# Gate and up projections of a gated MLP by Strassen's seven-product scheme, one Trainium2 core

## The chip, the cores and the metric

One core of a Trainium2 chip runs one launch. The metric is device time in microseconds (us), median of the runs shown. Engines are named as the profile names them: PE (matrix multiply; its weight loads are PEld), DVE (vector), ACT (scalar, activations), POOL (GpSimd), SP (the queue that issues every DMA here). `L326` is line 326 of the kernel before.

## The reference, cut to what matters

A transformer block with modulated layer norms: attention over 2048 queries, then a gated MLP. All values are float32. With D = 576, F = 4608 and 2048 tokens:

```python
mod = (silu(c) @ w_mod).reshape(1, 6, 1, -1)      # sa, ca, ga, sb, cb, gb
h = layernorm(x) * (1 + ca) + sa
x = x + ga * attention(h, k_cache, v_cache, wq, wo)  # 32 heads, 16 kv heads, last 512 keys
h = layernorm(x) * (1 + cb) + sb
gate = h @ W_gate                                  # (2048, 576) @ (576, 4608)
up = h @ W_up
x = x + gb * ((gate * (gate > 0) * up) @ W_down)
```

## The kernel before

**Precision.** PE multiplies in fp32r, a float32 format cut short. Every operand is therefore kept as two parts, hi (a cast on ACT) and lo (the rest, a subtraction on POOL), and a product is made as hi·hi + hi·lo + lo·hi, accumulated in PSUM. `split` (L173, L174) does this for weights.

**Projections.** `proj_ops` (L326) lists the matmuls of one 128 x 512 result (128 features, 512 tokens) with D = 576 as contraction: four tiles of 128 rows, three matmuls each, and the last 64 rows, whose hi and lo lie one above the other, in two. That is 14 matmuls of 512 columns. The operand of one 512-token block is `hT[qb]`, nine 512-column tiles in one buffer.

**Attention.** 128 units `u`, each one head and 512 queries. One unit's stages are written out by hand in the loop at the end, with steps of other work (`step(name, t, fn)`, due times shifted by the table `PLAN`) run between them. PE, DVE, ACT and POOL keep the order of the program. `T.*` and `woT*` are the last unit's leftovers, after `e = 10 * NU`. `b0` to `b3` are the second layer norm of the four 512-token blocks: statistics, norm on ACT, transposes on PE (L284), and `affine`, which writes hi and lo straight into `hT`.

**MLP.** 72 units `m`: 18 pairs of 128-feature tiles (`g`) by 4 token blocks (`qb`). `glu_pieces` makes gate and up of two feature tiles (4 x 14 matmuls) in eight pieces; the last piece of each feature tile also takes the PSUM pair out: relu on ACT (L540), times up on DVE (L541), hi cast on ACT (L544), lo on POOL (L545). The down projection of the unit before runs between: `md_piece` calls `down_piece` (L501), 12 matmuls of 288 columns for one 128-token tile into `psW`, which has one buffer of two banks, and a DVE add into `acc` (L507). There are four such pieces to a unit, one behind each of the pieces 3 to 6:

```python
for i in range(8):
    if pcs:
        pcs[i]()
    if 3 <= i <= 6 and m > 0:
        md_piece(m - 1, i - 3)
```

The first MLP pieces run among the leftovers of attention, from the due time `e + MLP0`. Weights are loaded whole (one DMA for a 128-feature tile, `prep5`, L181), cut once, and used for four token blocks. PSUM: `psS` two pairs of banks, `psW` one pair, `psM` two single banks.

Of the kernel before, what the change touches and what calls it, by code (L numbers as in the profile page):

```python
# [26 lines left out]
PLAN = {'a1.st0': -14, 'a1.nm0': -15, 'a1.st1': -14, 'a1.nm1': -15, 'a1.st2': -14, 'a1.nm2': -15, 'a1.st3': -14, 'a1.nm3': -15, 'a1.rs': -15, 'a1.tr0': -15, 'a1.af0': -11, 'a1.tr1': -15, 'a1.af1': -15, 'a1.tr2': -15, 'a1.af2': -15, 'a2.tr2': -1, 'wo2.g': 2, 'a3.st0': -10, 'a2.st2': -10, 'wq2.c': 4, 'wo2.l': -2, 'wo2.c': -2, 'mods': -3, 'k1.l': -5, 'k1.c': -8, 'b3.st0': 9, 'b3.nm0': 4, 'b3.st1': 8, 'b3.nm1': 5, 'b3.st2': 1, 'b3.nm2': 2, 'b3.st3': 5, 'b3.nm3': 3, 'b3.rs': 4, 'b3.tr0': 4, 'b3.af0': 14, 'b3.tr1': 3, 'b3.af1': 7, 'b3.tr2': 4, 'b3.af2': 4, 'b2.st1': 6, 'woT-1.3': 5, 'b0.st2': 6, 'b1.st0': 6, 'b1.st1': 0, 'b1.st2': 5, 'b1.st3': 0, 'b1.rs': 4, 'woT-1.1': 6, 'b2.st0': 0, 'b2.af0': 2, 'b0.st0': 15, 'b0.st1': 4, 'b0.st3': 6, 'b1.nm0': 0, 'b1.tr1': -3, 'b2.tr2': -3, 'b0.rs': 4, 'b1.af1': 2, 'T.olo2': 1, 'b1.nm1': 7, 'gb': -12, 'wu0.l': -4, 'wu0.c': 4, 'wu1.l': -14, 'T.ohi2': 0, 'b1.nm3': 4, 'wu1.c': 2, 'b2.st3': 1, 'woT-3.1': 2, 'b2.nm1': 3, 'wg0.c': -4, 'wg1.l': -3, 'b1.nm2': -2, 'b2.nm2': 1, 'wg0.l': -3, 'b2.af1': 5, 'wd1.g': -4, 'woT-3.2': -6, 'wd1.c': -2, 'T.pv1': -4, 'b2.st2': -1, 'T.pv0': -3, 'b1.af0': 1, 'b0.tr0': -1, 'wg1.c': 1, 'T.sum': -1, 'wd0.l': -1, 'b0.nm0': 1, 'b0.nm1': 6, 'b0.nm2': 0, 'b0.nm3': 1, 'b2.nm3': 2}  # L27
CFG = {'a3': (('m', 'aav', 'vap'), ('w', 'vvv', 'aav'), ('w', 'vvp')), 'a2': (('m', 'aav', 'vvv'), ('w', 'vvv', 'vvv'), ('s', 'aap')), 'a0': (('s', 'vvp', 'vvv'), ('m', 'aap', 'avp'), ('w', 'aav')), 'a1': (('w', 'aap', 'vap'), ('m', 'vvp', 'vvv'), ('s', 'avp')), 'b2': (('m', 'aav', 'avp'), ('s', 'aap', 'vvv'), ('w', 'vap')), 'b0': (('w', 'aav', 'avv'), ('m', 'aav', 'avv'), ('s', 'vap')), 'b1': (('s', 'vav', 'avp'), ('m', 'aap', 'vvv'), ('s', 'avp')), 'b3': (('m', 'vvp', 'vvv'), ('s', 'avv', 'avp'), ('s', 'vap'))}
# [4 lines left out]
def kernel(  # L33
# [19 lines left out]
    hp = ctx.enter_context(tc.tile_pool(name="hp", bufs=NQB))  # L53
# [9 lines left out]
    psM = ctx.enter_context(tc.tile_pool(name="psM", bufs=2, space=bass.MemoryType.PSUM))  # L63
    psW = ctx.enter_context(tc.tile_pool(name="psW", bufs=1, space=bass.MemoryType.PSUM))

# [10 lines left out]
    # quad[p, j] = 1 where p and j agree modulo 32; mask[p, a] = 1 where p // 32 == a  # L76
# [10 lines left out]
    # minus[p, j] = -1 in the rows 0 and 16, which carry the two parts of the maximum  # L87
# [116 lines left out]
    def prep_out(d, k, src, key):  # L204
        st = {}

        def load():
            st["raw"] = rp.tile([P, 640], F32, tag="raw", name=f"ro{key}_{k}")
            nc.sync.dma_start(st["raw"][:, :D], src[k])

        def gate():
            raw = st["gated"] = st["raw"][:, :D]
            nc.vector.tensor_tensor(raw, raw, mods[key], op=ALU.mult)

        def cut():
            raw = st["gated"]
            d[k] = wp.tile([P, 2, D], F32R, tag="wC", name=f"wo{key}_{k}")
            split(raw, D, d[k][:, 0, :], d[k][:, 1, :])

        return load, gate, cut  # L220
# [4 lines left out]
    hT = [None] * NQB  # L225

# [8 lines left out]
    class LayerNorm:  # L235
# [51 lines left out]
        def affine(self, ds, pool, tag, engs):  # L287
            qb = self.qb
            if not self.ready:
                hT[qb] = hp.tile([P, 9, 512], F32R, tag="hT", name=f"hT{self.key}_{qb}")  # L290
# [5 lines left out]
            for j, (d, e) in enumerate(zip(ds, engs)):  # L296
# [7 lines left out]
                out[d] = (h[:, 8, :], h[64:, 8, :]) if d == 4 else (h[:, d, :], h[:, 4 + d, :])  # L304
# [11 lines left out]
    def proj_ops(ps, w, h):  # L316
        ops = []
        for t in range(4):
            ops.append((w[:, t, :], h[:, t, :]))
            ops.append((w[:, 5 + t, :], h[:, t, :]))  # L320
        ops.append((w[:, 4, :], h[:, 8, :]))
        ops.append((w[:, 9, :], h[:, 8, :]))
        for t in range(4):
            ops.append((w[:, t, :], h[:, 4 + t, :]))
        n = len(ops)
        return [lambda i=i, a=a, b=b: nc.tensor.matmul(ps, a, b, start=(i == 0), stop=(i == n - 1))  # L326
                for i, (a, b) in enumerate(ops)]

# [189 lines left out]
    NG = NFT // 2  # L518
    MU = NG * NQB
    gs, us, ds_ = {}, {}, {}  # L520
    hhi, hlo = {}, {}

    def glu_pieces(m, j):
        g, qb = divmod(m, NQB)
        f = 2 * g + j
        st = {}

        def mm(which, w, lo, hi):
            if which == 0 and lo == 0:
                assert ready[qb] == "b"  # L530
                st["ps"] = psS.tile([P, 2, 512], F32, tag="s", name=f"gu{m}_{j}")
            if lo == 0:
                st["o"] = proj_ops(st["ps"][:, which, :], w[f], hT[qb])
            for fn in st["o"][lo:hi]:
                fn()

        def last():
            mm(1, us, 7, 14)
            r = bp.tile([P, 512], F32, tag="bc", name=f"relu{m}_{j}")
            nc.scalar.activation(r, st["ps"][:, 0, :], AF.Relu, bias=0.0, scale=1.0)  # L540
            nc.vector.tensor_tensor(r, st["ps"][:, 1, :], r, op=ALU.mult)  # L541
            hhi[m, j] = op.tile([P, 512], F32R, tag="ohi", name=f"hhi{m}_{j}")
            hlo[m, j] = op.tile([P, 512], F32R, tag="olo", name=f"hlo{m}_{j}")
            nc.scalar.copy(hhi[m, j], r)  # L544
            nc.gpsimd.tensor_sub(hlo[m, j], r, hhi[m, j].bitcast(F32))  # L545

        return [lambda: mm(0, gs, 0, 7), lambda: mm(0, gs, 7, 14),
                lambda: mm(1, us, 0, 7), last]

    def md_piece(m, qt):  # L550
        g, qb = divmod(m, NQB)
        down_piece([hhi[m, 0], hhi[m, 1]], [hlo[m, 0], hlo[m, 1]], [ds_[2 * g], ds_[2 * g + 1]],
                   4 * qb + qt, qt, f"md{m}_{qt}")()
        if g == NG - 1:
            i = 4 * qb + qt
            nc.sync.dma_start(out[i * P:(i + 1) * P, :], acc[i])

# [163 lines left out]
    prep("wd0", e + 20, prep_dn(0))  # L721
    prep("wd1", e + 26, prep_dn(1))
# [3 lines left out]
    norm_steps("b1", 1, "b", "wC", "raw", (e - 20, e - 14, e - 10, e - 4), e - 4, (e + 4,) * 4,  # L726
               (e + 14, e + 16, e + 19), (e + 14, e + 16, e + 19), sss)
    norm_steps("b2", 2, "b", "xm", "raw", (e + 4, e + 6, e + 10, e + 14), e + 16, (e + 20,) * 4,
               (e + 24, e + 26, e + 29), (e + 24, e + 26, e + 29), sss)
    norm_steps("b3", 3, "b", "xm", "raw", (e + 16, e + 19, e + 20, e + 24), e + 26, (e + 30,) * 4,  # L730
               (e + 34, e + 36, e + 39), (e + 34, e + 36, e + 39), sss)
# [3 lines left out]
    def mat(m, i, fn):  # L735
        mextra.setdefault((m, i), []).append(fn)

    def mat2(m, i, pr):
        k = 8 * m + i - 2
        m, i = m + i // 8, i % 8  # L740
        mat(k // 8, k % 8, pr[0])
        if len(pr) > 2:
            mat((k + 1) // 8, (k + 1) % 8, pr[1])
        mat(m, i, pr[-1])

    for g in range(NG - 1):
        b = NQB * g
        late = 0 if g else 8
        mat2(b, 4 + late, prep_mlp(gs, wg, "wA", 2 * g + 2))
        mat2(b, 6 + late, prep_mlp(us, wu, "wB", 2 * g + 2))  # L750
        mat2(b + 1, 4 + (0 if g else 6), prep_dn(2 * g + 2))
        mat2(b + 3, 3, prep_mlp(gs, wg, "wA", 2 * g + 3))
        mat2(b + 3, 5, prep_mlp(us, wu, "wB", 2 * g + 3))
        mat2(b + 4, 7, prep_dn(2 * g + 3))

    def mlp_steps():
# [130 lines left out]
```

## Time and profile before

| | |
|---|---|
| median of 3 runs | 3090.31 us (3089.53 to 3090.82) |
| span of the profiled execution | 3088.5 us |
| time beside the span | 1.8 us between the span and the median |
| PE busy | 3005.2 us, 97% of the span |
| DVE, ACT, POOL busy | 60%, 34%, 58% |
| instructions | 39282 |

The profile is one execution, with times in us from the start of the span. The page gives busy time by engine, then the span in 40 slices, then the chain of work that ended last. The groups of instructions give the mean duration of one; the timeline gives start and duration of each run of like instructions, with the idle time before it and what ended that idle time in brackets. Matmuls are pipelined, so the step from one start to the next, and not the duration shown, is what a matmul costs PE.

### The profile page before, as it was taken

Reading aid. Unit: us, or ns where it says so; the run is one execution under the profiler, and the core shown is the slowest. Engines: PE = TensorE matmul, PEld = TensorE weight load, DVE = VectorE, ACT = ScalarE, POOL = GpSimd, SP = SyncE. Lnnn points to the kernel's source line nnn. Section 1 sums busy time; section 2 is a strip of 40 time slices with the busy share of each in tenths; the row PEclk is TensorE's granted clock in tenths of the full one; section 3 lists DMA queues with packets and bytes.
Section 4 is the critical chain, followed back from the end, with each engine's and each line's share of the span. In section 5 each row is a group of like instructions: output and inputs, shape, how many; then the busy total and the mean of one; then the engine's idle time right before and its main releaser. Section 6 shows DMA issues by size and latency. Waiting matters only on the chain.

```text
span 3088.5 us, 39282 instructions
## 1 busy us (share of the span) xinstructions
PE 3005.2 (97%) x15918; PEld 2598.8 (84%) x15918; DVE 1853.5 (60%) x2633; ACT 1039.6 (34%) x1378; POOL 1805.7 (58%) x1177
## 2 busy tenths in 40 slices
PE   6899999999999999999998999999999999999998
PEld 4688888888888888888886888888888888888887
DVE  7888888888888989888887322222222222222222
ACT  5444444444444444444445311111111111111111
POOL 5788998888988898889986322222222222222221
PEclk9999999999999999999999999999999999999998
DMA  3000000000000000000000100000000000000001
GB/s 138 28 16 17 19 20 27 24 23 28 23 20 23 28 23 24 16 20 20 20 15 11 30 26 25 25 26 25 28 27 27 28 25 25 25 25 25 25 13 62
DMA packets 37765, 83.33 MB, mean 27 GB/s; under 512 B 4304, under 2 KB 4304, under 8 KB 37584
## 3 DMA queue, kind: packets, MB, share of 16 engines
q1 hardware_dynamic: 37584, 80.83, 8.7%
q8 instruction: 125, 2.05, 0.3%
q14 instruction: 56, 0.46, 0.0%
HBM read 76.09 MB, written 4.72 MB: 26 GB/s over the span
## 4 chain that ended last, share of the span: by engine, by line
PE 88%; DVE 9%; issue 1%; ACT 1%; POOL 0%; DMA 0%; SPq 0%; POOLq 0%; DVEq 0%; ACTq 0%
PE gu L326 29%; PE md L501 15%; PE wo L501 13%; PE qps L326 7%; PE s L375 4%; PE s L374 4%; PE s L373 4%; PE pv L473 4%; PE pv L474 4%; PE pv L475 3%; DVE t L378 2%; DVE t L386 2%; DVE t L392 1%; PE qm L399 1%; DVE t L385 1%
## 5 line engine op out<-in xcount | busy, mean ns | idle before, releaser
L545 POOL TENSOR_TENSOR hlo<-relu,hhi 128x512 fp32r<-128x512 f32 x144 | 186.5, 1295 | 993.9 <-ACT hhi L544 993.9
L455 POOL TENSOR_TENSOR lo<-p,hi 128x1024 fp32r<-128x1024 f32 x256 | 608.9, 2399 | 0.0
L507 DVE TENSOR_TENSOR acc<-md,acc 128x576 f32<-128x576 f32 x288 | 218.2, 758 | 517.8 <-PE md L501 517.8
L326 PE MATMUL gu<-hTb,wA 128*128 128x512 f32 x2016 | 495.9, 391 | 2.5 <-DVE relu L541 2.5
L326 PE MATMUL gu<-hTb,wB 128*128 128x512 f32 x2016 | 495.8, 391 | 0.0
L501 PE MATMUL md<-wogb,hhi 128*128 128x288 f32 x2304 | 467.4, 296 | 4.3 <-DVE acc L507 2.5
L326 PEld LDWEIGHTS gu<-hTb,wA 128*128 128x128 f32 x2016 | 370.7, 188 | 73.4 <-DVE relu L541 3.2
L326 PE MATMUL qps<-hTa,wA 128*128 128x512 f32 x1792 | 430.5, 391 | 2.0 <-DVE hTa L310 1.1
L501 PE MATMUL wo<-woga,ohi 128*128 128x288 f32 x2048 | 426.2, 301 | 3.9 <-DVE acc L507 2.3
L326 PEld LDWEIGHTS gu<-hTb,wB 128*128 128x128 f32 x2016 | 370.8, 188 | 69.9
L540 ACT ACTIVATE relu<-gu 128x512 f32<-128x512 f32 x144 | 86.2, 599 | 968.6 <-PE gu L326 968.6
L501 PEld LDWEIGHTS md<-wogb,hhi 128*128 128x128 f32 x2304 | 387.0, 189 | 28.7 <-DVE acc L507 3.5
L464 POOL TENSOR_TENSOR ks<-ks,p 128x512 f32<-128x512 f32 x256 | 345.1, 1348 | 95.5 <-ACT p L448 81.9
L326 PEld LDWEIGHTS qps<-hTa,wA 128*128 128x128 f32 x1792 | 338.7, 189 | 73.6 <-ACT hTa L310 1.5
L541 DVE TENSOR_TENSOR relu<-gu,relu 128x512 f32<-128x512 f32 x144 | 99.7, 692 | 498.0 <-ACT relu L540 498.0
L378 DVE TRANSPOSE_TENSOR_REDUCE t<-s 128x32 f32<-128x1024 f32 x256 | 319.2, 1248 | 69.5 <-PE s L375 56.7
L501 PEld LDWEIGHTS wo<-woga,ohi 128*128 128x128 f32 x2048 | 332.9, 189 | 17.4 <-DVE acc L507 5.7
L501 PE MATMUL md<-wogb,hlo 128*128 128x288 f32 x1152 | 341.4, 296 | 0.8 <-POOL hlo L545 0.8
L448 ACT ACTIVATE p<-p 128x1024 f32<-128x1024 f32 x242 | 256.2, 1059 | 140.0 <-DVE p L446 108.4
L501 PE MATMUL wo<-woga,olo 128*128 128x288 f32 x1024 | 302.5, 295 | 0.0
L446 DVE TENSOR_TENSOR p<-s,mb 128x1024 f32<-128x1024 f32 x242 | 295.1, 1219 | 3.8
L435 ACT CAST hi<-p 128x1024 fp32r<-128x1024 f32 x256 | 270.3, 1056 | 8.0
(125 smaller groups left out, 4546.9 us busy)
## 6 DMA issues: line engine op xcount, KB each, us to landing
rwA<-wg SPq DMA_DIRECT2D x36, 320.0 KB, 2.8
rwB<-wu SPq DMA_DIRECT2D x36, 320.0 KB, 3.0
rogb<-wd SPq DMA_DIRECT2D x36, 288.0 KB, 2.8
rwA<-wq SPq DMA_DIRECT2D x32, 320.0 KB, 2.9
roga<-wo SPq DMA_DIRECT2D x32, 288.0 KB, 2.8
rkv<-kv SPq DMA_DIRECT2D x32, 256.0 KB, 2.6
acc<-x SPq DMA_DIRECT2D x16, 288.0 KB, 5.6
out<-acc SPq DMA_DIRECT2D x16, 288.0 KB, 2.1
```

Source lines behind the costliest of these rows:

```text
L326: return [lambda i=i, a=a, b=b: nc.tensor.matmul(ps, a, b, start=(i == 0), stop=(i == n - 1)) for i, (a, b) in enumerate(ops)]
L373: nc.tensor.matmul(ps, k[:, kt, :], qhi[u], start=True, stop=False)
L374: nc.tensor.matmul(ps, k[:, 4 + kt, :], qhi[u], start=False, stop=False)
L378: nc.vector.tensor_reduce(t4[u][:, 2 * h:2 * h + 2, :].rearrange("p k b -> p (k b)"), t.rearrange("p k (b j) -> p (k b) j", j=32), axis=AX ...
L435: nc.scalar.copy(hi_[u, h], pt[u, h])
L446: nc.vector.tensor_tensor(p, t, bc[u][:, None, :].to_broadcast([P, 2, 512]), op=ALU.subtract)
L448: nc.scalar.activation(p, p, AF.Exp, bias=0.0, scale=1.0)
L455: nc.gpsimd.tensor_sub(lo_[u, h], pt[u, h], hi_[u, h].bitcast(F32))
L464: nc.gpsimd.tensor_tensor(ks_[u], ks_[u], p[:, j, :], op=ALU.add)
L501: nc.tensor.matmul(ps[:, half, :H2], a[:, sl], w[:, b, cs], start=(n == 0), stop=(n == 5))
L507: nc.vector.tensor_tensor(av, ps[:, :, :H2], av, op=ALU.add)
L545: nc.gpsimd.tensor_sub(hlo[m, j], r, hhi[m, j].bitcast(F32))
```

## The change

The MLP is written anew; attention keeps its order. What is done now:

- Gate and up are computed in two passes `b` of 1024 tokens. A block `m` (36 of them, `NB`) takes two 128-feature tiles by 1024 tokens, so each of gate and up is a 2 x 2 grid of 128 x 512 results. D is cut in two halves of 288. Strassen's scheme (in Winograd's form, with shared sums) makes the grid from seven products in place of eight.
- A product `prod(m, s)` has 7 matmuls for gate and 7 for up: two tiles of 128 rows in three matmuls each, and one of 96 rows, in which the 32 leftover rows stand three times for hi·hi, hi·lo and lo·hi. The results of products 0 and 1, and of 5 and 6, share one PSUM pair: the second is added onto the first there.
- The sums of weight blocks (`w_prep`, DVE) and their hi and lo parts (`w_split`) are made for each of the 36 blocks, three products ahead (`LEAD`), from raw weights that `w_load` brings with ten DMAs for each of four blocks. The sums of the token operand (`h_comb`) and their splits (`h_split`) are made once for each pass, in `h_steps`.
- The second layer norm writes its plain float32 output to a DRAM scratch `hb`, and `h_load` reads it back in the layout of the halves. Token blocks 0 and 1 are normed at the end of attention; 2 and 3 in four `ln_half` steps inside blocks 2, 4, 6 and 8, over `psW`.
- `evac(m, s)` takes a product out of PSUM: product 0 by an ACT copy into `q`, 1 by relu and product as before, 2 to 6 by a DVE add with `q` or `r`; behind 4, 5 and 6 a DVE `scalar_tensor_tensor` (relu times up, both from SBUF) and `h_out` (hi on ACT, lo on POOL).
- `md_piece` is unchanged inside; there are eight to a block, two behind product 0 and one behind each other.
- The MLP begins when all leftovers of attention are done. A third PSUM pair `psX` takes the place of `psM` there.

The core of the diff:

```diff
-    hp = ctx.enter_context(tc.tile_pool(name="hp", bufs=NQB))
+    hp = ctx.enter_context(tc.tile_pool(name="hp", bufs=9 * NQB))
...
+            if self.key == "b":
...
+                    nc.sync.dma_start(hb[qb, d][:n], f[:n])
+                return
...
+    def w_load(m, i, j):
+        fp = m % NFP
+        t = wraw[m, i, j] = pp.tile([P, 2, 3, P], F32, tag=RAW[i, j], name=f"wr{m}_{i}{j}")
+        for xx, src in enumerate((wg, wu)):
+            f = src[2 * fp + i]
+            nc.sync.dma_start(t[:, xx, 0:2, :].rearrange("p t n -> p (t n)"),
+                              f[:, 256 * j:256 * j + 256])
+            for r in range(4):
+                nc.sync.dma_start(t[32 * r:32 * r + 32, xx, 2, :], f[32 * j:32 * j + 32, 512:640])
...
+    def w_split(n, raw):
+        w = wop[n] = wp.tile([P, 2, 5, P], F32R, tag="wB" if n % 4 == 3 else "wA", name=f"wop{n}")
+        nc.scalar.copy(w[:, :, 0:3, :], raw)
+        nc.gpsimd.tensor_sub(w[0:32, :, 2, :], raw[0:32, :, 2, :], w[0:32, :, 2, :].bitcast(F32))
+        nc.gpsimd.tensor_sub(w[:, :, 3:5, :], raw[:, :, 0:2, :], w[:, :, 0:2, :].bitcast(F32))
...
+        elif s == 1:
+            w_split(n, r[0, 1])
+            s1 = wraw[m, "s1"] = pp.tile([P, 2, 3, P], F32, tag="hi", name=f"ws1_{m}")
+            nc.vector.tensor_tensor(flat(s1), flat(r[1, 0]), flat(r[1, 1]), op=ALU.add)
+            nc.vector.tensor_tensor(flat(r[1, 0]), flat(r[0, 0]), flat(r[1, 0]), op=ALU.subtract)
...
+    def prod(m, s, first):
+
+        hs, w = hop[m // NFP, s], wop.pop(7 * m + s)
+        for xx in range(2):
+            ps = pair[m][:, xx, :]
+            ops = []
+            for t in range(2):
+                ops += [(w[:, xx, t, :], hs[t]), (w[:, xx, 3 + t, :], hs[t]), (w[:, xx, t, :], hs[3 + t])]
+            ops.append((w[0:96, xx, 2, :], hs[2][0:96]))
+            for i, (a, c) in enumerate(ops):
+                nc.tensor.matmul(ps, a, c, start=first and i == 0, stop=i == len(ops) - 1,
+                                 skip_group_check=True)
...
+    def gated(m, f, k, c):
+        nc.vector.scalar_tensor_tensor(c[:, 0, :], c[:, 0, :], 0.0, c[:, 1, :], op0=ALU.max, op1=ALU.mult)
+        h_out(m, f, k, c[:, 0, :])
...
+        if s == 0:
+            t = tmp["q"] = pp.tile([P, 2, 512], F32, tag="hi", name=f"q{m}")
+            nc.scalar.copy(t, ps)
...
+        elif s == 5:
+            nc.vector.tensor_tensor(tmp["r"], ps, tmp["r"], op=ALU.add)
+            gated(m, 1, 1, tmp["r"])
...
+    def mlp_all():
+        for ij in RAW:
+            w_load(0, *ij)
+        for n in range(LEAD):
+            w_prep(n)
+        for m in range(NB):
+            md = [(k, qt) for k in range(2) for qt in range(4)] if m else []
+            for s in range(-1, 7):
+                if s >= 0:
+                    if s in (0, 2, 3, 4, 5):
+                        new_pair(m)
+                    prod(m, s, s not in (1, 6))
+                    for k, qt in md[:1 if s else 2]:
+                        md_piece(m - 1, k, qt)
+                    md = md[1 if s else 2:]
+                    evac(m, s)
+                    w_prep(7 * m + s + LEAD)
+                for fn, *args in mextra.pop((m, s), []):
+                    fn()
+        for k in range(2):
+            for qt in range(4):
+                md_piece(NB - 1, k, qt)
...
+    psM_scope.__exit__(None, None, None)
+    px["x"] = ctx.enter_context(tc.tile_pool(name="psX", bufs=1, space=bass.MemoryType.PSUM,
+                                             reuse_waits="tile"))
+    mlp_all()
```

The splits and sums of the token operand stand in `mextra`: for the first pass at block 0 (before product 0 up to product 4), for the second at block 17 (products 1 to 6) and block 18 (products 0 and 1).

More of the change, by code (lines that the diff above doesn't have):

```diff
@@ L202, in prep_kv, with prep_out @@
         return load, cut
-    def prep_out(d, k, src, key):
+    def prep_out(d, k, src, key, slot=None, at=(None, "wC")):
         st = {}
+        slot = k if slot is None else slot
         def load():
@@ L225 @@
     hT = [None] * NQB
+    hb = {(qb, d): dr.tile([64 if d == 4 else P, 512], F32, name=f"hb{qb}_{d}")
+          for qb in range(NQB) for d in range(5)}
     pend = []
@@ L515, in wo_piece @@
                           4 * qb + qt, qt, f"wo{u1}_{qt}", mid)
[L518 to L555, printed above, removed]
-            nc.sync.dma_start(out[i * P:(i + 1) * P, :], acc[i])
+    NFP = NFT // 2
+    NB = 2 * NFP
+    ds_, hhi, hlo = {}, {}, {}
+    wop, wraw, hop = {}, {}, {}
+    pair, tmp = {}, {}
+    def md_piece(m, k, qt):
+        b, fp = divmod(m, NFP)
+        i = 8 * b + 4 * k + qt
+        down_piece([hhi[m, f, k] for f in range(2)], [hlo[m, f, k] for f in range(2)],
+                   [ds_[m, f] for f in range(2)], i, qt, f"md{m}_{k}_{qt}")()
+        if fp == NFP - 1:
+            nc.sync.dma_start(out[i * P:(i + 1) * P, :], acc[i])
@@ new lines, with h_load, h_split @@
+    hraw = {}
+    def h_load(b, j, k, where):
+        qb = 2 * b + k
+        for t in range(3):
+            pool, tag, w = where[t]
+            r = pool.tile([P, w], F32, tag=tag, name=f"hr{b}_{j}{k}{t}")[:, :512]
+            hraw[b, j, k, t] = r
+            if t < 2:
+                nc.sync.dma_start(r, hb[qb, 2 * j + t])
+            else:
+                for q in range(3):
+                    nc.sync.dma_start(r[32 * q:32 * q + 32], hb[qb, 4][32 * j:32 * j + 32])
+    def h_split(b, s, rs, engs):
+        hs = hop[b, s] = [hp.tile([P, 512], F32R, tag="hT", name=f"hop{b}_{s}_{k}") for k in range(5)]
+        for t in range(3):
+            n = 96 if t == 2 else P
+            nc.scalar.copy(hs[t][:n], rs[t][:n])
+        for t in (0, 1, 2):
+            eng = nc.vector if engs[t] == "v" else nc.gpsimd
+            if t < 2:
+                eng.tensor_sub(hs[3 + t], rs[t], hs[t].bitcast(F32))
+            else:
+                eng.tensor_sub(hs[2][64:96], rs[2][64:96], hs[2][64:96].bitcast(F32))
@@ new lines, in ln_half, with stats, norm, trans @@
+    def ln_half(qb, hh):
+        ts = [4 * qb + 2 * hh, 4 * qb + 2 * hh + 1]
+        st, xn = {}, []
+        nm = f"lh{qb}_{hh}"
+        cols = slice(256 * hh, 256 * hh + 256)
+        def stats():
+            mv = st["mv"] = sp.tile([P, 4, 2], F32, tag="mv", name=f"mv{nm}")
+            for i, t in enumerate(ts):
+                assert adds[t] == HQ // 2
+                bn = sp.tile([P, 2, 6], F32, tag="st", name=f"st{nm}_{i}", bufs=1)
+                for h in range(2):
+                    nc.vector.bn_stats(bn[:, h, :], acc[t][:, h * H2:(h + 1) * H2])
+                nc.vector.bn_aggr(mv[:, i, :], bn)
+            rs = st["rs"] = sp.tile([P, 2, 4], F32, tag="rs", name=f"rs{nm}")
+            nc.gpsimd.tensor_scalar(rs[:, 0, :2], mv[:, :2, 1], EPS, None, op0=ALU.add)
+            nc.gpsimd.tensor_tensor(rs[:, 0, :2], rs[:, 0, :2], mhalf[:, :2], op=ALU.pow)
+            nc.gpsimd.tensor_tensor(rs[:, 1, :2], mv[:, :2, 0], rs[:, 0, :2], op=ALU.mult)
+            nc.gpsimd.tensor_scalar(rs[:, 1, :2], rs[:, 1, :2], -1.0, None, op0=ALU.mult)
+        def norm():
+            for i, t in enumerate(ts):
+                pool, tag = ((rp, "raw"), (xp, "xm"))[i]
+                n = pool.tile([P, 640], F32, tag=tag, name=f"xn{nm}_{i}")
+                nc.scalar.activation(n[:, :D], acc[t], AF.Identity, bias=st["rs"][:, 1, i:i + 1],
+                                     scale=st["rs"][:, 0, i:i + 1])
+                xn.append(n)
+        def trans(ds):
+            ps = psW.tile([P, 2, 512], F32, tag="w", name=f"lt{nm}_{ds[0]}")
+            ps = ps.rearrange("p a (b n) -> p (a b) n", b=2)
+            p = 64 if ds[0] == 4 else P
+            if ds[0] == 4:
+                f = hp.tile([P, 512], F32, tag="hT", name=f"lf{nm}_4").rearrange("p (a n) -> p a n", a=2)
+            else:
+                f = wp.tile([P, 4, 256], F32, tag="wC", name=f"lf{nm}_0")
+            for j, d in enumerate(ds):
+                for i in range(2):
+                    nc.tensor.transpose(ps[:p, j, i * P:(i + 1) * P], xn[i][:, d * P:d * P + p], ident)
+            add, mul = mods["b"]
+            for j, d in enumerate(ds):
+                nc.scalar.activation(f[:p, j, :], ps[:p, j, :], AF.Identity, bias=add[:p, d:d + 1],
+                                     scale=mul[:p, d:d + 1])
+                nc.sync.dma_start(hb[qb, d][:, cols], f[:p, j, :])
+        return [stats, norm, lambda: trans((0, 1, 2, 3)), lambda: trans((4,))]
@@ new lines, with h_out @@
+    HI = {(0, 0): (op, "ohi"), (1, 0): (op, "ohi"), (1, 1): (bp, "bc"), (0, 1): (bp, "bc")}
+    def h_out(m, f, k, r):
+        pool, tag = HI[f, k]
+        hi = hhi[m, f, k] = pool.tile([P, 512], F32R, tag=tag, name=f"hhi{m}_{f}{k}")
+        if k == 0:
+            pool, tag, w = op, "olo", 512
+        elif f == 1:
+            pool, tag, w = qp, ("qlo", "qhi")[m % 2], 512
+        else:
+            pool, tag, w = xp, "xm", 640
+        lo = hlo[m, f, k] = pool.tile([P, w], F32R, tag=tag, name=f"hlo{m}_{f}{k}")[:, :512]
+        nc.scalar.copy(hi, r)
+        nc.gpsimd.tensor_sub(lo, r, hi.bitcast(F32))
@@ L559, with wd_prep @@
+    def wd_prep(m, f):
+        return prep_out(ds_, 2 * (m % NFP) + f, wd, "gb", (m, f), (None, "wB" if f else "wC"))
     pq0 = prep5(wqs, 0, wq, "wA")
@@ L733 @@
-    mextra = {}
[L735 to L754, printed above, removed]
@@ L756, in mlp_steps @@
-    def mlp_steps():
-        for m in range(MU + 1):
-            pcs = glu_pieces(m, 0) + glu_pieces(m, 1) if m < MU else []
-            for i in range(8):
-                if pcs:
-                    pcs[i]()
-                if 3 <= i <= 6 and m > 0:
-                    md_piece(m - 1, i - 3)
-                for fn in mextra.pop((m, i), []):
-                    fn()
-                yield
-    mlp = mlp_steps()
+    norm_steps("b1", 1, "b", "wC", "raw", (e - 14, e - 13, e - 6, e - 4), e - 3, (e - 2,) * 4,
+               (e + 1, e + 2, e + 4), (e + 1, e + 2, e + 4), sss)
@@ new lines, with mat @@
+    mextra = {}
+    def mat(m, s, fn, *args):
+        mextra.setdefault((m, s), []).append((fn,))
+    for m in range(NB):
+        for f in range(2):
+            pr = wd_prep(m, f)
+            for k in range(3):
+                mat(m, 3 * f + k, pr[k])
+    for i in range(4):
+        for s, fn in enumerate(ln_half(2 + i // 2, i % 2)):
+            mat(2 + 2 * i, s, fn)
+    LEAD = 3
+    h0 = h_steps(0, [(bp, "bc", 512), (wp, "wC", 512), (hp, "hT", 512)], [(hp, "hT", 512)] * 3)
+    h1 = h_steps(1, [(xp, "xm", 640), (wp, "wC", 512), (hp, "hT", 512)], [(hp, "hT", 512)] * 3)
@@ L776, in run @@
             fn(*args)
-        if k in HOOK and t >= e + MLP0:
-            next(mlp)
     run(-1, 9)
```

148 lines of the change are left out of this document (118 added, 30 removed).

## The prediction

> **What bounds the kernel now.** I read the page first, then the chain in order of time, then the groups of instructions, and the timeline where the change works.
>
> ```profile
> span 3088.5 us, 39282 instructions
> PE 3005.2 (97%) x15918; PEld 2598.8 (84%) x15918; DVE 1853.5 (60%) x2633; ACT 1039.6 (34%) x1378; POOL 1805.7 (58%) x1177
> PE   6899999999999999999998999999999999999998
> PE 88%; DVE 9%; issue 1%; ACT 1%; POOL 0%; DMA 0%; SPq 0%; POOLq 0%; DVEq 0%; ACTq 0%
> ```
>
> PE is the bound nearly everywhere. In the MLP (from about 1720 us) it is never idle, and the other engines are loaded lightly, as the row of one stretch shows (busy time of PE, PEld, DVE, ACT, POOL); the chain repeats every 19.12 us, once for each MLP unit (32 steps between its two rows: 611.83 / 32):
>
> ```profile
> 2500.00:3060.00 560.00, 560.00 (x3052) 493.62 (x3051) 145.17 (x190) 96.51 (x157) 134.35 (x98) 1.00 0.09 26
> ...
> 1918.60 7.96 PE gu L326 x35
> ...
> 2530.43 7.96 PE gu L326 x35
> ```
>
> What a matmul costs is read from starts: 14 and 14 matmuls of 512 columns, then 12 of 288, then the next:
>
> ```profile
> 3048.12 3.33 PE L326 MATMUL gu<-hTb,wA 128*128 128x512 f32 x14
> 3051.30 3.34 PE L326 MATMUL gu<-hTb,wB 128*128 128x512 f32 x14
> 3054.47 0.42 PE L501 MATMUL md<-wogb,hhi 128*128 128x288 f32 x2
> 3056.05 1.77 PE L326 MATMUL gu<-hTb,wA 128*128 128x512 f32 x7
> ```
>
> (3054.47 - 3048.12) / 28 = 0.227 us for a wide one, 1.58 us for the 12 of a down piece.
>
> **The change, part by part.**
>
> *Matmuls.* Two old units (2 feature tiles by 1024 tokens) had 2 x 56 = 112 wide matmuls and 8 down pieces, 38.24 us. A block has 7 x 14 = 98 and the same 8 pieces: 14 x 0.227 = 3.18 us less, 35.06 us. Over 36 blocks the gain is 114 us. No row shows a matmul on 96 rows (14 of the 98); bounds are 0 and 0.227 us, and I take 0.227, since all rows of that width cost that. [...]
>
> *Two down pieces in a row (behind product 0).* `psW` is one pair of banks, so the second waits for the first's DVE add. Before, seven wide matmuls always lie between. Only the tail shows the bare case:
>
> ```profile
> 3071.78 0.29 PE L501 MATMUL md<-wogb,hlo 128*128 128x288 f32 x1
> 3072.11 0.76 DVE L507 TENSOR_TENSOR acc<-md,acc 128x576 f32<-128x576 f32 x1 [3.29 <-PE md L501]
> 3072.92 0.50 PEld L501 LDWEIGHTS md<-wogb,hhi 128*128 128x128 f32 x2 [1.08 <-DVE acc L507]
> 3072.92 0.85 PE L501 MATMUL md<-wogb,hhi 128*128 128x288 f32 x2 [0.85 <-DVE acc L507]
> ...
> 3077.02 0.85 PE L501 MATMUL md<-wogb,hhi 128*128 128x288 f32 x2 [0.85 <-DVE acc L507]
> ```
>
> From the last start 3071.78 the next could come at 3071.91 and comes at 3072.92: 1.01 us lost. It covers product 0's ACT copy, which product 1 needs (1.02 us for such a copy, below).
>
> *Product 6 behind product 5.* Product 6 adds onto the bank pair that `evac` of product 5 must first read. In the program the DVE has, ahead of that read, the add of the down piece behind product 5. So PE finishes product 5 and its down piece, then waits for the add (0.33 us to its start, 0.76) and the 128 x 1024 read. Then it goes on. Price of the reads, and of the other work:
>
> ```profile
> L446 DVE TENSOR_TENSOR p<-s,mb 128x1024 f32<-128x1024 f32 x242 | 295.1, 1219 | 3.8
> L507 DVE TENSOR_TENSOR acc<-md,acc 128x576 f32<-128x576 f32 x288 | 218.2, 758 | 517.8 <-PE md L501 517.8
> L545 POOL TENSOR_TENSOR hlo<-relu,hhi 128x512 fp32r<-128x512 f32 x144 | 186.5, 1295 | 993.9 <-ACT hhi L544 993.9
> L455 POOL TENSOR_TENSOR lo<-p,hi 128x1024 fp32r<-128x1024 f32 x256 | 608.9, 2399 | 0.0
> L174 POOL TENSOR_TENSOR wogb<-rogb,wogb 128x576 fp32r<-128x576 f32 x36 | 52.0, 1444 | 26.1 <-ACT wogb L173 26.0
> L444 ACT ACTIVATE p<-s 128x1024 f32<-128x1024 f32 x14 | 14.3, 1022 | 3.7 <-PE s L442 3.7
> ```
>
> 0.33 + 0.76 + 1.22 + 0.05 to PE's start, less the 0.13 us of the last matmul's own slot: 2.2 us. Lower bound 0 (if the read were done during the 1.58 us piece), upper 2.2 plus whatever DVE still has from product 4 (about 1.5). I take 2.25.
>
> So a block costs 35.06 + 1.01 + 2.25 = 38.3 us, against 38.24 before: **the matmuls saved come back as two waits.**
>
> *Does anything else bind in a block?* POOL: seven `w_split` at 1.30 + 0.74 (256 columns, on the line through 512 and 1024 columns), four `h_out` at 1.30, two `wd` cuts at 1.44: 22.4 us. DVE: eight adds 6.1, five reads 6.1, the relu product 0.7, three gated products of 512 about 2.2, four weight sums of 768 columns at 1.0 (0.75 x 768 / 576), two `wd` gates 1.5: 20.6. ACT about 11. But DVE operations with two SBUF inputs exclude POOL, as these rows show: the same gating takes 0.75 us alone and 1.82 beside a POOL subtraction that started 0.08 us earlier:
>
> ```profile
> 2014.91 0.75 DVE L213 TENSOR_TENSOR rogb<-rogb,mrow 128x576 f32<-128x576 f32 x1
> 2024.45 1.82 DVE L213 TENSOR_TENSOR rogb<-rogb,mrow 128x576 f32<-128x576 f32 x1
> 2024.37 1.29 POOL L545 TENSOR_TENSOR hlo<-relu,hhi 128x512 fp32r<-128x512 f32 x1 [3.67 <-ACT hhi L544]
> ```
>
> Such DVE work is 7.7 us a block, so the pair is held 30 of 38 us. Weight parts are three products ahead (about 14 us), so I count this at nothing; followed by hand, the next block's ACT copy of product 0, which waits for the last POOL subtraction of `q`, ends about 0.7 us before PE needs it. That is thin, and if it goes PE waits at product 1.
>
> *DMAs.* SP issues 40 for weights and 2 for `wd` in a block:
>
> ```profile
> 1.17 1.84 SPq L103 DMA_DIRECT2D acc<-x  x4
> 2020.73 0.33 SPq L181 DMA_DIRECT2D rwA<-wg  x1
> rwA<-wg SPq DMA_DIRECT2D x36, 320.0 KB, 2.8
> ```
>
> 0.33 us alone, 0.46 in a run: 42 take 14 to 19 us of 38. Hidden in a block, but not at the start. A 32-row DMA is not in the trace; 0.33 is taken.
>
> *Start of the MLP.* Before, gate and up matmuls fill the leftovers of attention from 1674.94 us:
>
> ```profile
> 1665.30 0.50 PE L473 MATMUL pv<-hi,kv 128*128 128x512 f32 x1 [3.37 <-ACT lfb L308]
> 1665.64 0.50 PE L474 MATMUL pv<-hi,kv 128*128 128x512 f32 x1
> 1665.94 0.63 PE L475 MATMUL pv<-lo,kv 128*128 128x512 f32 x1
> ...
> 1674.94 1.77 PE L326 MATMUL gu<-hTb,wA 128*128 128x512 f32 x7
> ...
> 1698.43 0.98 PE L284 MATMUL ltb<-ident,xnb 128*128 128x128 f32 x7 [2.62 <-ACT xnb L266]
> ```
>
> After, the leftovers run bare (the last four `wo` pieces from about 1677, 2.6 us each with the psum wait, to 1688), and the first product needs weights and `hb`. SP issues the layer norm's stores by about 1675, then 40 weight DMAs (13 to 18 us) and five of `h_load` (2), then 2.8 to land, three ACT casts and the splits (4): product 0 starts near 1700 (1690 to 1712). Block 0 has PE work of only 22 us, but 12 sums, 11 DVE and 10 POOL splits of the token operand fall in it, in the same exclusive pair: from product 0 on, about 20 us of DVE and 30 of POOL, of which some goes into block 1. Its products follow these: 45 us (30 to 55).
>
> *Second pass, norms, tail.* In blocks 17 and 18 the same 23 DVE operations (15 us) and 10 of POOL (13) come on top of 30 held of 38 us: 28 - 17 free = 11, and two sums wait for loads issued just ahead of them, about 4 us each: 20 us lost (5 to 45). The `ln_half` steps: four times two transposes behind a down piece (1.01 us each) and ten transposes at 0.12 (2.41 / 20), 13 us:
>
> ```profile
> 1657.43 2.41 PE L284 MATMUL ltb<-ident,xnb 128*128 128x128 f32 x20 [0.85 <-DVE acc L507]
> ```
>
> The tail has eight bare pieces in place of four. The rows above step 4.10 us apart, with PE's clock lowered by then (0.24 us a matmul); two at 2.6, six at 4.1, and 3.3 from the last add to the end: 33 us (25 to 38).
>
> *Sum.* 1700 + 45 + 35 x 38.3 + 20 + 13 + 33 = 3152, against the span of 3088.5; with the 1.8 us between span and median, **3154 us**.
>
> **Rivals.**
>
> *Product 6 does not wait (faster).* If the read of product 5 ends within its down piece, a block costs 36.1 us: 35 x 2.25 = 79 us less, 3075. With my other terms the change breaks even where the waits of a block come to (3088.5 - 1700 - 45 - 20 - 13 - 33) / 35 - 35.06 = 1.4 us. For it: DVE is only half busy. Against: the order in the program, add before read, and DVE starting its work in order in every row I read. 0.10.
>
> *The ends cost little (no change).* Start 1690, block 0 30, second pass 5, tail 25: 48 us less, 3106; with 0.4 us less in each block it is within 0.2% (6 us either side, what a measurement of this kernel can tell) of before. 0.07, and 0.03 for landing below.
>
> *DVE and POOL fall behind.* If queueing for the pair adds 2.7 us a block, at product 1 or by late weight parts, 95 us more: 3250. For it: 30 of 38 us held and 0.7 us of slack. Against: three products of lead. 0.13.
>
> *PE's clock drops.* After 3.37 us idle the rows at 1665 show matmuls 0.43 us apart where 0.227 is usual, from 1665.94 on for about 3.5 us, 1.7 us lost; after 2.62 us (1698.43) they don't; in the tail idle times of 0.85 keep it low. If 2.2 us of waiting did so in each block: 35 x 1.7 = 60, 3214. 0.08. [...]
>
> *SP is the bound.* If the small DMAs cost 1 us each, 42 us a block: 36 x 3.7 = 133 more, 3285. Against: 0.33 in the row. 0.04.
>
> **How the numbers follow.** My forecast, slower, 3154, with its own range of 3115 to 3205, has 0.55. With the three slower rivals (0.13, 0.08, 0.04) slower has 0.80; within 0.2% 0.07; faster 0.10 + 0.03. The range 3075 to 3235 reaches to the wait's absence below and to half of the backlog above.
>
> **What would show it.** 98 x 36 = 3528 wide matmuls in place of 4032; PE idle before product 6 of some 2 us, ended by a DVE read of a bank pair, and before the second down piece of 0.85, ended by the add; a period of 38.3 us; a first product near 1700 and idle slices there and near the middle of the MLP. Wrong would be a period under 37 us, or a wait ended by POOL, ACT or a DMA in each block.

## The result, and the profile after

The changed kernel takes 3217.8 us against 3089.9, 128 us slower; the ratio on record is 1.0419, 95% interval 1.0404 to 1.0434. The forecast was 3154, slower by 64, and the measured time lies above its range of 3115 to 3205.

The page after: span, busy time by engine, PE's busy share and granted clock in 40 slices, the chain that ended last by engine.

```profile
span 3218.2 us, 41842 instructions
PE 2971.4 (92%) x15414; PEld 2546.9 (79%) x15414; DVE 2278.4 (71%) x3013; ACT 1193.1 (37%) x1562; POOL 2280.8 (71%) x1663
PE   6899999999999999999976999999996899999998
PEclk9999999999999999999998999999997999999999
PE 79%; DVE 13%; issue 2%; SPq 2%; POOL 1%; ACT 1%; DMA 1%; DVEq 0%; ACTq 0%; POOLq 0%
```

PE has 504 matmuls fewer and is busy 34 us less, and the span is 130 us longer: the MLP has idle time on PE in every block (the waits below), with much of it at two places, its start and its middle, and the chain runs through DVE for 13% where it was 9%.

The waits in the MLP, after, from 1700 to 3200 us (engine, line, whom it waited for: us in total, times, longest):

```profile
PE gu L728 <- DVE r L780: 84.4, 36, 7.6
PE md L520 <- DVE acc L526: 54.7, 42, 9.9
DVE hr L636 <- DMA hr<-hb: 11.7, 3, 10.5
```

L780 is the DVE read of product 5: once in each of the 36 blocks product 6 waits for it. The timeline of PE and DVE, after: the start, that place in two blocks, and the second of two down pieces in a row:

```profile
1700.17 1.22 PE L728 MATMUL gu<-hop,wop 128*128 128x512 f32 x2 [5.18 <-ACT hop L625]
...
1787.37 3.46 PE L728 MATMUL gu<-hop,wop 128*128 128x512 f32 x14 [2.07 <-DVE r L780]
...
2155.29 0.76 DVE L526 TENSOR_TENSOR acc<-md,acc 128x576 f32<-128x576 f32 x1 [1.53 <-PE md L520]
2155.97 1.22 DVE L780 TENSOR_TENSOR r<-gu,r 128x1024 f32<-128x1024 f32 x1
2157.33 5.04 PE L728 MATMUL gu<-hop,wop 128*128 128x512 f32 x14 [2.07 <-DVE r L780]
...
3159.59 0.53 PE L520 MATMUL md<-wogb,hhi 128*128 128x288 f32 x2 [0.85 <-DVE acc L526]
```

The reader sees the add (2155.29) ahead of the read (2155.97), and PE's 2.07 us. After the same wait the 14 matmuls take 3.46 us in one block and 5.04 in the other. In the second, PE's clock was halved for part of the time, as the two stretches show (length, busy PE, PEld, DVE, ACT, POOL; PE's granted clock, DMA share, GB/s):

```profile
1787.37:1790.83 3.46, 3.46 (x16) 2.87 (x17) 3.39 (x3) 1.93 (x3) 2.14 (x2) 1.00 0.00 0
2157.33:2162.37 5.04, 5.04 (x16) 4.01 (x17) 3.38 (x3) 1.93 (x3) 3.73 (x3) 0.66 0.00 0
```

The clock records of this profile show one stretch of 3.41 us at half clock, a low window, in 19 of the 28 blocks without norms or operand sums (the plain blocks). The time from one ACT copy of product 0 to the next is called the period below. In the plain blocks it is about 38.7 us without a low window (9 of them) and 40.3 us with one (19).

### The profile page after: what moved, and what is told of

The parts are those of the page before. It is cut to its first block, busy times and chain, and to the rows that moved or that the text cites. A ratio compares the mean times of both kernels' runs of the same rounds, so it can differ in the third digit from the quotient of the medians.

```text
span 3218.2 us, 41842 instructions
## 1 busy us (share of the span) xinstructions
PE 2971.4 (92%) x15414; PEld 2546.9 (79%) x15414; DVE 2278.4 (71%) x3013; ACT 1193.1 (37%) x1562; POOL 2280.8 (71%) x1663
## 4 chain that ended last, share of the span: by engine, by line
PE 79%; DVE 13%; issue 2%; SPq 2%; POOL 1%; ACT 1%; DMA 1%; DVEq 0%; ACTq 0%; POOLq 0%
PE gu L728 24%; PE md L520 14%; PE wo L520 12%; PE qps L345 7%; PE s L394 4%; PE s L393 4%; PE s L392 4%; PE pv L492 3%; PE pv L493 3%; PE pv L494 3%; DVE t L397 2%; DVE acc L526 2%; DVE t L405 2%; DVE t L411 1%; DVE r L780 1%
## 5 line engine op out<-in xcount | busy, mean ns | idle before, releaser
L728 PE MATMUL gu<-hop,wop 128*128 128x512 f32 x3528 | 903.6, 409 | 102.3 <-DVE r L780 84.4
L728 PEld LDWEIGHTS gu<-hop,wop 128*128 128x128 f32 x3528 | 680.9, 197 | 253.4 <-issue 83.0
L520 PE MATMUL md<-wogb,hhi 128*128 128x288 f32 x2304 | 476.3, 299 | 59.0 <-DVE acc L526 59.0
L573 POOL TENSOR_TENSOR wop<-wr,wop 128x512 fp32r<-128x512 f32 x216 | 275.4, 1275 | 0.0
L744 POOL TENSOR_TENSOR hlo<-r,hhi 128x512 fp32r<-128x512 f32 x72 | 93.8, 1302 | 253.6 <-ACT hhi L743 247.7
L744 POOL TENSOR_TENSOR hlo<-c,hhi 128x512 fp32r<-128x512 f32 x36 | 47.5, 1320 | 278.2 <-ACT hhi L743 278.2
L504 ACT CAST ohi<-rb 128x512 fp32r<-128x512 f32 x128 | 79.2, 619 | 407.0 <-PE wo L520 402.6
L508 POOL TENSOR_TENSOR olo<-rb,ohi 128x512 fp32r<-128x512 f32 x128 | 170.1, 1329 | 68.9 <-ACT ohi L504 68.9
```

What stands on the lines that cost most here:

```text
L508: nc.gpsimd.tensor_sub(olo[u], o.pop(u), ohi[u].bitcast(F32))
L520: nc.tensor.matmul(ps[:, half, :H2], a[:, sl], w[:, b, cs], start=(n == 0), stop=(n == 5))
L573: nc.gpsimd.tensor_sub(w[:, :, 3:5, :], raw[:, :, 0:2, :], w[:, :, 0:2, :].bitcast(F32))
L728: nc.tensor.matmul(ps, a, c, start=first and i == 0, stop=i == len(ops) - 1, skip_group_check=True)
```

## The experiments

**The read ahead of the add.**

```diff
                     prod(m, s, s not in (1, 6))
+                    if s == 5:
+                        evac(m, s)
                     for k, qt in md[:1 if s else 2]:
                         md_piece(m - 1, k, qt)
-                    evac(m, s)
+                    if s != 5:
+                        evac(m, s)
```

> Behind product 5 the DVE read of its banks (and the gated product) is issued ahead of the down piece's add; all else as in the changed kernel. Theory A (the add ahead of the read makes PE wait 2.07 us at product 6, and this gap itself brings PE's clock down for one 3.4 us window in about two blocks of three, 1.6 us each): the wait at product 6 goes (under 0.3 us), only 0.85 us a block is left, no low-clock windows in the plain blocks, the period falls from 38.74 and 40.30 to 36.7 us; 3218 - 35 x 2.05 - 22 x 1.57 = 3112 (3100 to 3125). Rival B (DVE and POOL are behind in any case, the wait only moves to the copy of product 0 or to late weight parts): the period stays over 38 us, 3160 to 3200.

Measured: 3182.4 us, ratio 1.0306 (1.0291 to 1.0322). The wait at product 6 and the low-clock windows of the plain blocks are gone (granted clock over the span 0.982, against 0.972 in the changed kernel), but the period (second pass) is 38.5 us, not 36.7. Half of A holds, and B is right on the time. Most of the 35 us gained is the clock: a plain block at full clock went from 38.7 to 38.5 us only, while 19 low windows, 30 us, are gone. Timeline of DVE, POOL and PE in one block:

```profile
2725.61 0.74 DVE L526 TENSOR_TENSOR acc<-md,acc 128x576 f32<-128x576 f32 x1
2726.25 1.28 POOL L573 TENSOR_TENSOR wop<-wr,wop 128x512 fp32r<-128x512 f32 x1
2726.28 4.01 DVE L588 TENSOR_TENSOR ws<-wr,wr 128x768 f32<-128x768 f32 x1
2727.50 1.27 POOL L744 TENSOR_TENSOR hlo<-r,hhi 128x512 fp32r<-128x512 f32 x1
2728.74 0.73 POOL L572 TENSOR_TENSOR wop<-wr,wop 32x256 fp32r<-32x256 f32 x1
2730.32 3.31 DVE L589 TENSOR_TENSOR wr<-wr,wr 128x768 f32<-128x768 f32 x1
2733.55 0.74 DVE L526 TENSOR_TENSOR acc<-md,acc 128x576 f32<-128x576 f32 x1
2734.36 0.53 PE L520 MATMUL md<-wogb,hhi 128*128 128x288 f32 x2 [1.05 <-DVE acc L526]
2737.75 0.53 PE L520 MATMUL md<-wogb,hhi 128*128 128x288 f32 x2 [1.54 <-DVE acc L526]
```

Two weight sums of 768 columns stand 4.01 and 3.31 us on DVE, while POOL runs subtractions one behind another; the add of product 6's down piece comes only then, and the next down piece waits for it. The groups of instructions show the same sum in the changed kernel and here:

```profile
L588 DVE TENSOR_TENSOR ws<-wr,wr 128x768 f32<-128x768 f32 x36 | 34.3, 952 | 0.4
```
```profile
L588 DVE TENSOR_TENSOR ws<-wr,wr 128x768 f32<-128x768 f32 x36 | 143.9, 3997 | 0.0
```

0.95 us against 4.0. In the changed kernel the sum came later, after the read that PE waited for, and found POOL idle, as in the block from 1757.75:

```profile
1785.87 1.26 POOL L573 TENSOR_TENSOR wop<-wr,wop 128x512 fp32r<-128x512 f32 x1
1787.87 0.95 DVE L588 TENSOR_TENSOR ws<-wr,wr 128x768 f32<-128x768 f32 x1
1788.69 1.29 POOL L744 TENSOR_TENSOR hlo<-r,hhi 128x512 fp32r<-128x512 f32 x1 [1.57 <-ACT hhi L743]
```

**Also no two down pieces in a row, and this alone.** The first of the two pieces moves between the gate and up halves of product 0.

```diff
         for xx in range(2):
+            if xx and mid:
+                md_piece(m - 1, *mid)
             ps = pair[m][:, xx, :]
```

> As read_first, and the first of the two down pieces behind product 0 is moved between its gate and up halves, so that no two down pieces stand in a row. A: the second wait of 0.85 us (1.0 us of issue) goes as well, period 35.7 us, 3112 - 35 = 3077 (3065 to 3092), under the kernel before. B: product 1 then waits for the ACT copy of product 0, whose cover is gone; the time stays within 10 us of read_first.

Measured: 3195.4 us, ratio 1.0349 (1.0332 to 1.0366), 13 slower than read_first, which neither A nor B had. One wait of up to 2.7 us for the add replaces the two of 1.05 and 1.54, and low-clock windows return (periods 38.6 and 39.6). PE does not wait for the copy of product 0 in the plain blocks; it waits for the late add.

> Only the down piece moved between the halves of product 0; product 6 waits as before. A: 1.0 us a block less, 35 us, and the gap of 2.07 us stays and with it low-clock windows in some share of the blocks: 3183 (3165 to 3200). B (the piece was the needed cover of product 0's copy): within 10 us of the changed kernel.

Measured: 3165.8 us, ratio 1.0249 (1.0234 to 1.0265): 52 us gained where A said 35 (the time is inside A's range, at its lower end). The second wait is gone, the wait at product 6 is as it was (PE's waits in one stretch of 440 us: the changed kernel, then this one):

```profile
PE gu L728 <- DVE r L780: 22.8, 11, 2.1
PE md L520 <- DVE acc L526: 9.4, 11, 0.9
```
```profile
PE gu L730 <- DVE r L782: 22.8, 11, 2.1
```

The period is 37.6 us, and in the second pass a low-clock window falls in 1 of 16 blocks in place of 11.

**The read in two halves.**

```diff
-            nc.vector.tensor_tensor(tmp["r"], ps, tmp["r"], op=ALU.add)
+            for xx in range(2):
+                nc.vector.tensor_tensor(tmp["r"][:, xx, :], ps[:, xx, :], tmp["r"][:, xx, :], op=ALU.add)
```

> Order as in the changed kernel, but the DVE read of product 5 is made in two of 512 columns, gate's bank first, so that the gate matmuls of product 6 can start after the first. The wait should shrink from 2.07 to about 1.5 us: 35 x 0.53 = 19 us. What it tells apart is the clock: if the low-clock windows come from a gap that fills most of a window of 3.4 us, a gap of 1.5 us brings none and a further 34 us go: 3165 (3155 to 3178). If any gap of an us or more can bring them, they stay: about 3199 (3190 to 3208).

Measured: 3221.6 us, ratio 1.0432 (1.0417 to 1.0448); neither of the two expected gains came. The gap was not shortened: PE waits for both halves.

```profile
2708.51 1.28 DVE L781 TENSOR_TENSOR r<-gu,r 128x512 f32<-128x512 f32 x2
2709.94 5.03 PE L728 MATMUL gu<-hop,wop 128*128 128x512 f32 x14 [2.14 <-DVE r L781]
```

So it says nothing on the length of gap that lowers the clock.

**The phase of the gap.**

```diff
             for i, (a, c) in enumerate(ops):
+                if s in (2, 3, 4) and xx == 0 and i == 0:
+                    nc.tensor.matmul(ps, a, c, start=True, stop=False, skip_group_check=True)
```

> split_only with the first gate matmul of products 2, 3 and 4 issued twice (0.68 us of PE work more in a block, same result). split_only has the same wait of 2.07 us at product 6 as the changed kernel, but its period of 37.6 us is 11 times 3.41 us, and low-clock windows came in 4 of 35 blocks only. If the clock is judged in windows of 3.41 us that run freely, and a gap lowers it only where it falls into one window, the new period of 38.3 us moves the gap through the window and low clock returns in four to seven blocks of ten: 3166 + 24 + 14 to 24 x 1.57 = 3212 to 3228. If split_only was spared for another reason, only the added work shows: 3190 (3185 to 3196).

Measured: 3191.2 us, ratio 1.0333 (1.0319 to 1.0347): 25 us over split_only, so by its total only the added 24 us show and the expectation missed. By blocks, second pass: periods of 38.3 us and, in 6 of 16 blocks, 39.8 or 39.9, against 1 of 16 in split_only. In the first pass, where the blocks with norms break the rhythm, 5 of the 12 plain blocks have a long period in either kernel (39.1 or 39.2 us in split_only, 39.7 to 39.9 here), and the four blocks with norms took 176.3 us in split_only and 170.9 here, which evens most of it out: the granted clock over the span is 0.977 and 0.978. So split_only was not spared as far as the expectation says: 6 of its 28 plain blocks have the long period.

What decides can be read from the clock records of the changed kernel. All 76 begin at multiples of 3.413 us from the first, to within 4 ns, as do the 16 of the kernel before; a window is one such step. Take PE's idle time (the gaps of over 0.05 us between matmuls) in every window of the plain blocks. Of the windows at full clock, the 19 that were followed by a low one held 1.97 to 2.08 us of idle time, and the 289 others held 1.88 us at most. The gap of 2.07 us before 1787.37 lies across a border, 1.22 us on one side and 0.85 on the other; the one before 2157.33 lies in one window, and the next window is low. So in this trace the place of the gap does decide, as the expectation had it. Outside the plain blocks, where other matmuls run, the border is less sharp: 1.69 us was enough once (the kernel before, the window at 3068.65) and 1.965 was not (the changed kernel, at 1656.8).

**Weight sums left out, or moved.** First read_first_split with the four sums of each block deleted (its output is then not the reference's); then with all four kept and the two behind product 5 made behind product 3:

```diff
-            s1 = wraw[m, "s1"] = pp.tile([P, 2, 3, P], F32, tag="hi", name=f"ws1_{m}")
-            nc.vector.tensor_tensor(flat(s1), flat(r[1, 0]), flat(r[1, 1]), op=ALU.add)
-            nc.vector.tensor_tensor(flat(r[1, 0]), flat(r[0, 0]), flat(r[1, 0]), op=ALU.subtract)
...
         else:
             w_split(n, r[0, 1])
+            if m + 1 < NB:
+                w_sums(m + 1)
```

> As read_first_split, with the four DVE weight sums of each block left out (so the weights are not Strassen's, and the output is not the reference's). In read_first and read_first_split two of these sums, 0.95 us alone, took 4.0 and 3.3 us behind POOL work, and the down piece's add behind them held PE. Theory A2 (DVE operations with two SBUF inputs lose the shared pair to POOL's queue): waits of the down pieces on adds vanish, period 35.7 us with no low-clock windows, 3195 - 33 x 3.4 = 3083 (3070 to 3100). Rival (DVE is late for other reasons, its order or its total): the period stays over 37.5 us, 3150 or more.

Measured: 3066.3 us, ratio 0.9925 (0.9910 to 0.9940), period 35.6 us, no wait of a down piece on an add in the plain blocks, no low-clock window there. What A2 forecast came, and the time lies 4 us below its range; what DVE and POOL share is A2's guess, which no run shows.

> As read_first_split, with the two weight sums of the first part moved from behind product 5 to behind product 3, where POOL has only one weight split, and the load that they need one product earlier. Nothing is left out. A2: they take 1 to 2 us there, where no add is due for 3 us; the add behind product 6 comes in time; period 36 us (35.7 to 36.5), 3195 - 33 x 3.1 = 3093 (3080 to 3110). Rival: the total load of the pair counts, not the place; the period stays over 37.5.

Measured: 3126.4 us, ratio 1.0120 (1.0102 to 1.0139), period 35.9 to 37.7, 16 us above A2's range. The period falls with nothing left out, so the total load of DVE and POOL does not forbid the gain; but product 6 waits again, up to 1.9 us. The timeline of all_moves, the run below that has this edit and the next one, shows why:

```profile
2711.91 0.96 DVE L581 TENSOR_TENSOR ws<-wr,wr 128x768 f32<-128x768 f32 x1 [2.51 <-DMA wr<-wu]
2712.91 0.96 DVE L582 TENSOR_TENSOR wr<-wr,wr 128x768 f32<-128x768 f32 x1
2718.34 3.46 PE L737 MATMUL gu<-hop,wop 128*128 128x512 f32 x14 [1.24 <-DVE r L789]
```

The sums run in 0.96 us now, but DVE waited 2.51 us for the load, and its delay reaches the read of product 5.

**The loads.**

```diff
-    for m, s, names in ((NFP - 1, 1, "l11 l21 s0"), (NFP - 1, 2, "s1"), (NFP - 1, 3, "l12 t1"),
-                        (NFP - 1, 4, "l22 t3 t2"),
+    for m, s, names in ((NFP - 1, 1, "l11 l21 s0"), (NFP - 1, 2, "l12"), (NFP - 1, 3, "l22 s1"),
+                        (NFP - 1, 4, "t1 t3 t2"),
```

> The changed kernel, with two of the second pass's loads issued one product earlier (and its first sum a product later), so that they don't stand behind the twenty weight DMAs of product 3 and 4 on SP. In the changed kernel a sum waited 10.6 us for such a load with an add behind it, and PE stood twice for about 8 to 10 us. If that queueing is the cause: the long block falls from 64.5 to about 50 us, 3218 - 15 = 3203 (3195 to 3210). If the pair of DVE and POOL is full there anyway: no change within 5 us.

Measured: 3209.9 us, ratio 1.0389 (1.0373 to 1.0404). The long block (17, where the second pass's operands are made) falls from 64.5 to 55.4 us, where 50 was expected; the queue of SP is the cause of that part. In the changed kernel SP and DVE show it: the load (2436.26) stands behind ten weight DMAs that had waited for their buffer to 2431.08, and the sum, with an add behind it, waits for the load.

```profile
2431.08 0.35 SPq L564 DMA_DIRECT2D wr<-wg  x1
2436.26 0.84 SPq L616 DMA_DIRECT2D hr<-hb  x2
2438.83 0.69 DVE L636 TENSOR_TENSOR hr<-hr,hr 128x512 f32<-128x512 f32 x1 [10.55 <-DMA hr<-hb]
2453.63 4.61 PE L728 MATMUL gu<-hop,wop 128*128 128x512 f32 x10 [7.59 <-DVE r L780]
```

> read_first_split, sums_early and mid_early together. A2 with the loads as cause of the middle: 3093 - 15 = 3078 (3065 to 3095), 0.3% under the kernel before. Rivals: as in the parts, 3150 or more.

Measured: 3116.6 us, ratio 1.0096 (1.0079 to 1.0113). As sums_early, less 10 us, and 22 us above the expected range.

The last edit lays gate and up weights out so that one DMA brings all of a raw half block:

```diff
-            nc.sync.dma_start(t[:, xx, 0:2, :].rearrange("p t n -> p (t n)"),
-                              f[:, 256 * j:256 * j + 256])
-            for r in range(4):
-                nc.sync.dma_start(t[32 * r:32 * r + 32, xx, 2, :], f[32 * j:32 * j + 32, 512:640])
+            nc.sync.dma_start(t[:, xx, :, :].rearrange("p t n -> p (t n)"),
+                              f[:, 384 * j:384 * j + 384])
```

> The changed kernel, with the gate and up weights laid out so that each raw block comes with one DMA for gate and one for up (2 in place of 10; the 32 leftover rows lie four times in the input). If SP's 0.45 us for each DMA is what makes the first product late, the middle's sum wait and the weights come late: start 8 to 12 us earlier, the middle 10 to 15 us shorter, plain blocks unchanged (their waits are not on loads): 3218 - 22 = 3196 (3188 to 3203). If the issues were hidden: no change within 5 us.

Measured, on the changed kernel alone: 3211.4 us, ratio 1.0401 (1.0385 to 1.0417). The first copy of product 0 comes 4.7 us earlier, the long block is 5.7 us shorter, the plain blocks as they were. The expected 22 us did not come: the issues cost less there than expected.

> all_moves with the same weight layout. In all_moves the weight sums behind product 3 waited 2.5 us for a load queued behind thirty others, and product 6 then waited 1.2 us for DVE. If that is what is left over the 35.6 us of no_sums: period 35.8, 33 x 1.0 less, start and middle 15 to 20 less: 3117 - 50 = 3067 (3055 to 3080), 0.7% under the kernel before. If it is the pair of DVE and POOL: period stays over 36.5, 3095 to 3105.

Measured: 3064.9 us, ratio 0.9926 (0.9913 to 0.9938): **0.74% faster than the kernel before**, and inside the expected range. The period is 35.6 us. One stretch of the second pass, the changed kernel and this one (busy PE, PEld, DVE, ACT, POOL; PE's clock, DMA share, GB/s):

```profile
2540.00:2980.00 440.00, 407.84 (x2152) 354.61 (x2151) 226.67 (x254) 115.35 (x165) 244.33 (x220) 0.97 0.20 55
```
```profile
2540.00:2980.00 440.00, 440.00 (x2403) 387.41 (x2402) 257.52 (x285) 129.74 (x185) 271.48 (x247) 1.00 0.21 62
```

In this stretch PE has no idle time left, with DVE and POOL busier than in the changed kernel, at 59 and 62%.

## Why the prediction was right or wrong

The direction and its mechanism were right: the matmuls saved come back as two waits for DVE adds. By terms, in us of the span:

| term | forecast | measured | difference |
|---|---|---|---|
| product 0 of block 0 starts | 1700 | 1700.2 | 0 |
| block 0 | 45 | 53 | +8 |
| 28 plain blocks | 28 x 38.3 = 1072 | 1115 | +43 |
| 4 blocks with norms | 166 | 172 | +5 |
| blocks 17 and 18 | 97 | 114 | +18 |
| block 35 and tail | 71 | 64 | -7 |

**The matmuls.** 98 in 35.6 us of a block with its eight down pieces where nothing waits (no_sums, all_one_load), for 35.06 forecast. 0.4 us of the rest is at the changes from one group to the next, which I had as 0: a product takes 3.22 us and a piece 1.60, not 3.18 and 1.58. The matmuls on 96 rows cost as the others (median 0.233 us to the next start at full clock in the changed kernel, where the others have medians of 0.227 to 0.237).

**The two waits.** 1.0 and 2.2 us as forecast: a plain block at full clock is 38.7 us with both and 35.6 without (all_one_load). split_only takes the first away and read_first the second.

**The clock: the step that failed.** I gave "PE's clock drops" 0.08 and left it out of the sum. It came in 19 of 28 plain blocks at 1.57 us, 30 us, nearly half of what was missing; the group changes, 0.4 us in each, are the rest of the plain blocks' 43. The price I had (1.7 us) was right and the chance wrong. I took the row after 2.62 us idle, at full clock, as evidence that 2.2 us is harmless; it lay across a border of two windows, 0.68 us and 1.94. The tail's row could not have told either: before, the clock was already low from 3072.06, behind idle times of 1.73 and 0.82 us, and it stayed low through the waits of 0.85, while in the tail after, it stayed high through the same waits. In the plain blocks a low window followed the gap of 2.07 us in two of three, by where the gap fell (phase_shift).

**The middle.** Forecast 20 us lost, measured 34 to 38. I had two sums waiting about 4 us each for loads "issued just ahead of them"; one waited 10.55, since SP's own wait for a buffer stood ahead of the load. mid_early took 9 us of it. What the rest comes from stays open: in all_one_load the two blocks still take 54.2 and 46.3 us, 29 more than two plain ones. The operand sums and splits that fall there are the likely cause, not shown.

**The start, block 0 and the tail.** The start fell on the forecast partly by luck. I had all 40 weight DMAs behind the layer norm's stores, which were to be issued by 1675 us. The last store was issued near 1680, but half of the weight DMAs had gone out by 1666; with 8 in place of 40 (one_load) the first matmul starts 5.2 us earlier. Block 0 took 53 us, inside the bounds of 30 to 55. In the tail the clock stayed high and a piece took 2.7 us and not 4.1, near my lower bound.

**The rival on the other side** asked that product 6 not wait, and gave 3075. read_first did that and gained 35 us, not 79: I had counted the pair of DVE and POOL at nothing in a block. That was true only while PE waited. When the wait goes, the sums meet POOL's queue, and the rival "DVE and POOL fall behind" takes its place. Its cure need not be less work (no_sums): a place and a load in time do as well (sums_early, all_one_load). One sum was off by two: the rival "SP is the bound" gives 3154 + 133 = 3287, not 3285.

## What to carry to other kernels

Count a saving on the bound engine only after following, in program order, what each other engine has queued ahead of the instruction that frees its buffer: here one add ahead of one read gave back two thirds of the saving. When one wait is taken away, look at what it covered; the work that ran in its shadow is the next wait. A cheap sum that waits for a load or for another engine is dear when an add that frees PSUM is queued behind it, so place it where nothing is due, and get its load off a queue of small DMAs.

## What the runs showed of the hardware

- The clock records of the changed kernel lie on steps of 3.413 us (76 of 76). In its plain blocks each of the 19 steps that held 1.97 to 2.08 us of PE idle time was followed by one at half clock, and none of the 289 others at full clock, with 1.88 us or less, was. In the tail before, the clock was low from 3072.06 to the end, with waits of 0.85 us every 4.10.
- A DVE sum of two SBUF tiles took longer beside POOL: the one at 2726.28 (read_first) took 4.01 us, while three POOL instructions ran (2726.25, 2727.50, 2728.74), and ended 0.82 us after the last of them. In the changed kernel, with POOL idle, the same sum took 0.95 us. Why the two engines hold each other up is not shown.
- SP took 1.82 us to issue four DMAs of 32 rows and 16 KB (the changed kernel, at 1650.45), and 1.84 us for four of 288 KB (the kernel before, at 1.17): 0.46 us each.
